# Norm sums on GpSimd, an identity made without it, and a Softmax issued step by step, in a cross-covariance attention and feed-forward kernel

## The chip, the cores and the metric

The kernel runs on one core of a Trainium2 chip. The metric is the device time of one execution in microseconds. The kernel before takes 575.51 us in the median of 9 runs (575.19 to 575.95).

## What is computed

Four batches of q, k and v come in, each 5824 x 256 in float32. Every column of q and k is normalized over the 5824 tokens, a 256 x 256 Softmax matrix is made from them, v is multiplied with it, and a feed-forward part with one product of two branches follows. In short:

```python
qn = q / (np.linalg.norm(q, axis=1, keepdims=True) + 1e-06)
kn = k / (np.linalg.norm(k, axis=1, keepdims=True) + 1e-06)
s = kn.transpose(0, 2, 1) @ qn / tau          # tau = 1
a = softmax(s, axis=-1)                       # with 1e-09 added to the sum
x = (v @ a).reshape(B * N, 256)
h = (x @ w1) * (x @ w2)                       # 256 -> 1024, twice
out = (h @ w3) @ w_out                        # 1024 -> 1024 -> 256
```

## The kernel before

Nothing non-linear stands between the weights, so they are folded. W = w3 @ w_out is made once (`w_unit`, L572). For each batch the Softmax matrix is multiplied into w1 and w2 (`fold`, L355), which gives Wf, 256 x 1024 twice. What is left for each token is the pair of products a and b of its row of v with the two halves of Wf, their product abs, and the output o = abs @ W.

The main loop (L636 to L647) runs over batches, over 12 chunks of tokens (11 of 512, a last one of 192) and over 8 column blocks j. One turn is a round. `emit_ab` (L419) issues two matmuls of 512 columns into a tile a and two into a tile b; ScalarE casts a to bfloat16 (L431), DVE multiplies it with b (L440). `emit_out` (L450) issues the four o matmuls of an earlier round (LAG = 2). After the last j of a chunk ScalarE and DVE each copy half of o out of PSUM (L486, L487), and the result is stored from SyncE's queue.

PSUM is shared out by tags: "ab" has four banks, which a, b, the folds and the small sums take in turn, "out" has three for o, and "G" has one for the score matrix.

Between the rounds the work for the next batch is put in. `make_agenda` (L587) writes a list of due times, with a cost for each item, and `run_due` (L381) issues what is due against a clock that is advanced by the reckoned TensorE time of what has been issued. The items are these.

- Loads of q, k and v pieces. They go over GpSimd's queue with a conversion to bfloat16. Ahead of each stands a one-element copy on GpSimd (`gate` L410, `hold` L415) that waits for a product of the current round or for a transposed piece of v, so a load doesn't start before its time. v is then transposed by DMA from SyncE's queue (L155 and following).
- Score units of the next batch (`score_units`, L167): two slots of tokens at a time, squares of q and k on ScalarE (L185), the products G = q^T k on TensorE (L188), and the squares added up on DVE in float32 (`acc`, L197). At batch index 0 they are due from 58.0 to 120.0 on the clock, later from 16.0 to 104.0 (t0, t1).
- Softmax units of the next batch (`soft_units`, L239), which the change touches.

The Softmax units of batches two to four are: `norms` (L263), one addition on DVE that leaves the squares of q and k of each of 128 partitions; `k_row` (L269), a float32 matmul with a matrix of ones that sums k's squares over partitions and spreads the sums over all of them, and four ScalarE steps (L274 to L277: logarithm, half of it exponentiated, again for the reciprocal) that turn it into kr; `q_sums` (L280), four float32 matmuls of one column for q's sums, followed by `q_norm` (L289: two ScalarE steps, two on DVE) that gives the scale r; `scaled`, two DVE multiplications of G with kr (`scale`, L302) and two ScalarE exponentials with scale r (L307); `sums` (L323, L329), the row sums over partitions and their reciprocal rs; and eight folds of two matmuls each (L344), copied out alternately by ScalarE (L351) and DVE (L353). They are due at t1 + 1.0, 3.5, 4.0, 8.0, 12.0, and the folds from t1 + 13.0 on, 0.9 apart.

The first batch has no earlier batch to hide behind. Its squares are made on TensorE (`squares`, L213) while q and k come in; the diagonals are picked out with an identity matrix. The identity is made on GpSimd (L502, a memset and a select) between the first four loads and the next ones. TensorE runs dummy matmuls (`busy`, L205) ahead of the first data, 14 of them.

Each engine works through its own instructions in the order of issue, so what stands behind a waiting instruction waits too.

Of the kernel before, what the change touches and what calls it, by code (L numbers as in the profile page):

```python
# [7 lines left out]


# [2 lines left out]
ALU = mybir.AluOpType  # L12
# [12 lines left out]
def kernel(  # L25
# [213 lines left out]
    def soft_units(n):  # L239
        st = {}  # L240

        def k_first():
            d = work.tile([P, CT, P], F32, tag="sq", name="dk", bufs=2)
            nc.vector.tensor_mul(d, S["k"], ident.unsqueeze(1).to_broadcast([P, CT, P]))
            st["ksq"] = d.rearrange("p c t -> p (c t)")

        def q_first():
            d = work.tile([P, CT, P], F32, tag="sq", name="dq", bufs=2)
            ss = work.tile([P, CT], F32, tag="ss0", name="ss0", bufs=1)
            for ct in range(CT):  # L250
                nc.vector.tensor_tensor_reduce(
                    out=d[:, ct, :], in0=S["q"][:, ct, :], in1=ident, scale=1.0, scalar=0.0,
                    op0=ALU.mult, op1=ALU.add, accum_out=ss[:, ct : ct + 1],
                )
            st["ss"] = ss

        def scaled_first():
            scale(0)
            q_norm(st["ss"])
            scale(1)  # L260
            exps()

        def norms():  # L263
            a1 = work.tile([P, 2, C], F32, tag="acc1", name=f"acc1_{n}", bufs=1)
            nc.vector.tensor_add(a1, accs[n][:, 0], accs[n][:, 1])
            st["ksq"] = a1[:, 1, :]
            st["qsq"] = a1[:, 0, :]

        def k_row():  # L269

            m = psum.tile([P, 512], F32, tag="ab", name=f"row_{n}", bufs=4)
            nc.tensor.matmul(m[:, :C], lhsT=ones_pp, rhs=st["ksq"], start=True, stop=True)  # L272
            kr = work.tile([P, C], F32, tag="kr", name=f"kr_{n}", bufs=1)
            nc.scalar.activation(out=kr, in_=m[:, :C], func=AF.Ln)  # L274
            nc.scalar.activation(out=kr, in_=kr, func=AF.Exp, scale=0.5)  # L275
            nc.scalar.activation(out=kr, in_=kr, func=AF.Ln, bias=eps_t)  # L276
            nc.scalar.activation(out=kr, in_=kr, func=AF.Exp, scale=-1.0)  # L277
            st["kr"] = kr

        def q_sums():  # L280
            m = psum.tile([P, 512], F32, tag="ab", name=f"ss_{n}", bufs=4)
            for ct in range(CT):
                nc.tensor.matmul(
                    m[:, ct : ct + 1], lhsT=st["qsq"][:, ct * P : (ct + 1) * P], rhs=ones_f,
                    start=(ct == 0), stop=(ct == CT - 1), skip_group_check=True,
                )
            q_norm(m[:, :CT])

        def q_norm(src):  # L289
            r = work.tile([P, CT], F32, tag="r", name=f"r_{n}", bufs=2)  # L290
            nc.scalar.activation(out=r, in_=src, func=AF.Ln)
            nc.scalar.activation(out=r, in_=r, func=AF.Exp, scale=0.5)
            nc.vector.tensor_scalar_add(r, r, 1e-6)
            nc.vector.reciprocal(r, r)
            if inv_tau != 1.0:
                nc.vector.tensor_scalar_mul(r, r, inv_tau)
            st["r"] = r

        def scale(ct):
            if ct == 0:  # L300
                st["s"] = work.tile([P, CT, C], F32, tag="s", name=f"s_{n}", bufs=1)
            nc.vector.tensor_mul(st["s"][:, ct, :], G_tiles[n][:, ct, :], st["kr"])  # L302

        def exps():
            e = work.tile([P, CT, C], BF16, tag="e", name=f"e_{n}", bufs=2)
            for ct in range(CT):
                nc.scalar.activation(  # L307
                    out=e[:, ct, :], in_=st["s"][:, ct, :], func=AF.Exp, scale=st["r"][:, ct : ct + 1]
                )
            st["e"] = e  # L310

        def scaled():
            for ct in range(CT):
                scale(ct)
            exps()

        def sum_mm(c2):
            if c2 == 0:
                st["sum"] = psum.tile([P, 512], F32, tag="out" if n == 0 else "ab", name=f"sum_{n}", bufs=3 if n == 0 else 4)
# [12 lines left out]

        def sums():
            sum_mm(0)
            sum_mm(1)

        def fold_mm(i, c2, tag="ab", on_act=None):
            h, rest = divmod(i, 4)
            w, c1 = divmod(rest, 2)
            if c2 == 0:  # L340
                st["fold", i] = psum.tile(
                    [P, 512], F32, tag=tag, name=f"fold_{n}_{i}", bufs={"ab": 4, "out": 3}[tag]
                )
            nc.tensor.matmul(  # L344
                st["fold", i], lhsT=st["e"][:, c2, c1 * P : (c1 + 1) * P], rhs=w12[:, c2, w, h * 512 : (h + 1) * 512],
                start=(c2 == 0), stop=(c2 == CT - 1),
            )
            if c2 == CT - 1:
                dst = Wf[n][:, c1, w, h * 512 : (h + 1) * 512]
                if on_act if on_act is not None else i % 2 == 0:  # L350
                    nc.scalar.activation(out=dst, in_=st["fold", i], func=AF.Copy, scale=st["rs"][:, c1 : c1 + 1])  # L351
                else:
                    nc.vector.tensor_scalar_mul(dst, st["fold", i], st["rs"][:, c1 : c1 + 1])  # L353

        def fold(i, tag="ab", on_act=None):  # L355
            fold_mm(i, 0, tag)
            fold_mm(i, 1, tag, i % 2 == 0 if on_act is None else on_act)

        def first_folds():
            sum_mm(0)  # L360
            fold_mm(0, 0)
            fold_mm(1, 0)
            sum_mm(1)
            fold_mm(0, 1)
            fold_mm(1, 1)
            fold(2)
            transpose_half_on_pe(0, 0, 0, False)
            fold(3, on_act=True)
            fold(4, "out", on_act=False)
            fold(5, "out")  # L370

        if n == 0:
            return [k_first, k_row, q_first, scaled_first, first_folds] + [lambda i=i: fold(i) for i in range(6, 8)]
        head = [(0.0, norms), (0.5, k_row), (0.4, q_sums)]
        return head + [(0.0, scaled), (0.2, sums)] + [(0.43, lambda i=i: fold(i)) for i in range(8)]


    clock = [0.0]
# [11 lines left out]
    def at(t, cost, fn):  # L390
        seq[0] += 1
        agenda.append((t, seq[0], cost, fn))
# [106 lines left out]
    busy(14)  # L499
    load_piece("k", 0, 0, (half,))  # L500
    load_piece("q", 0, 0, (half,))
    masks.make_identity(nc, ident)  # L502
    nc.vector.tensor_copy(ident_b, ident)
    w3_wout = vT_pool.tile([P, (NT - 1) * C], BF16, tag="vT", name="w3_wout")
    w3_bf = w3_wout[:, : FT * F].rearrange("p (j l) -> p j l", l=F)
    wout_sb = w3_wout[:, FT * F : FT * (F + D)].rearrange("p (l d) -> p l d", d=D)
# [2 lines left out]
    def transpose_w3():  # L509

        for h in range(FT // 2):
            m = in_pool.tile([P, 2, FT, P], BF16, tag="k", name=f"w3T_{h}", bufs=IN_BUFS["k"])
            nc.sync.dma_start_transpose(m, w3_bf[:, 2 * h : 2 * h + 2, :])
            w3T.append(m)

    w3r = moe_w3.rearrange("(jh jl) l -> jl jh l", jl=P)
    w1r = moe_w1.rearrange("(ch cl) f -> cl ch f", cl=P)
# [54 lines left out]
    def w_unit(jt):  # L572
# [10 lines left out]
        if jt == FT - 1:  # L583
            w_ready[0] = True


    def make_agenda(b):  # L587
        agenda.clear()
# [2 lines left out]
        if b == 0:  # L591
            for i in range(2):
                at(1.5 + 0.6 * i, 0.43, soft0[5 + i])
            at(4.0, 0.5, lambda: transpose_half_on_pe(0, 0, 1, False))
            at(7.0, 0.5, lambda: transpose_half_on_pe(0, 1, 0, True))
            at(8.0, 0.5, lambda: transpose_half_on_pe(0, 1, 1, False))
# [4 lines left out]
            moves = [("v", 0, 3, 29.0), ("qk", 1, 0, 38.0), ("qk", 1, 1, 43.0), ("v", 0, 4, 50.0), ("qk", 1, 2, 58.0)]  # L601
            moves += [("qk", 1, 3, 63.0), ("v", 0, 5, 70.0), ("qk", 1, 4, 81.0), ("qk", 1, 5, 87.0)]
            moves += [("v", 1, 0, 96.0), ("v", 1, 1, 106.0), ("v", 1, 2, 116.0), ("qk", 2, 0, 126.0)]
            t0, t1 = 58.0, 120.0
        else:
            moves = [("v", b, 3, 1.0), ("qk", n, 1, 10.0), ("qk", n, 2, 17.0), ("v", b, 4, 26.0), ("qk", n, 3, 38.0)]
            moves += [("v", b, 5, 46.0), ("qk", n, 4, 58.0), ("qk", n, 5, 66.0)]
# [20 lines left out]
        for i, (cst, fn) in enumerate(units):  # L628
            at(t0 + (t1 - t0) * i / len(units), cst, fn)
        soft = soft_units(n)  # L630
        ts = [t1 + 1.0, t1 + 3.5, t1 + 4.0, t1 + 8.0, t1 + 12.0] + [t1 + 13.0 + 0.9 * i for i in range(8)]
        for t, (cst, fn) in zip(ts, soft):
            at(t, cst, fn)
        agenda.sort()

    for b in range(B):  # L636
# [48 lines left out]
```

## Time and profile before

| | |
|---|---|
| median of 9 runs | 575.51 us |
| profiled execution, its own time | 575.19 us |
| its span, first to last instruction | 573.4 us |
| granted TensorE clock | 0.999 |
| DVE busy / ScalarE busy / GpSimd busy | 65% / 59% / 13% |
| the cast of a (L431), one of 128 x 512 | 0.58 us |
| the product abs (L440), one of 128 x 512 | 0.69 us |
| k steps L274, L275, L276, L277 | 0.38, 0.42, 0.51, 0.42 us |
| an exponential L307 | 0.50 us |
| a multiplication of G with kr, L302 | 0.42 us |
| a fold copied out, ScalarE / DVE | 0.69 / 0.75 us |
| norms' addition L265 | 0.68 us |

The span counts from the first to the last instruction of the program; the execution's own time has 1.8 us more around it. A row of the order of time gives the start, the length, the engine, the line, the operation, the tiles written and read, and how many instructions of the kind follow one another; in brackets is the engine's idle time before it and what ended it. PE is TensorE, PEld its weight loads, ACT is ScalarE, POOL is GpSimd. The end of a matmul is modelled, so a gap of TensorE is read from the distance between the starts of matmuls, not from its busy time. In the chain of waits TensorE has 91% of the span, DMA 5%, which is the head, and every other engine 1% or less.

### The profile page before, as it was taken

What the parts mean: (1) busy time and instruction counts of PE and PEld (TensorE: products, weight loads), DVE (VectorE), ACT (ScalarE), POOL (GpSimd) and SP (SyncE); (2) the same over time, 40 slices, a digit from 0 to 9 for tenths busy, and PEclk for the clock granted to TensorE, in tenths of its full rate; (3) what the DMA queues carried; (4) which work ended last, traced back from release to release, by engine and by line L of the source; (5) the groups of instructions that cost most, each with busy time, mean ns of one, the idle gap of its engine ahead of it and who ended that gap; (6) DMA issues with size and microseconds to landing.
All of it is one profiled execution on the core that took longest, in us unless ns stands there. A gap on an engine that the chain in (4) does not pass through costs nothing.

```text
span 573.4 us, 10131 instructions
## 1 busy us (share of the span) xinstructions
PE 562.0 (98%) x3766; PEld 356.8 (62%) x3766; DVE 374.5 (65%) x597; ACT 337.9 (59%) x624; POOL 72.3 (13%) x162
## 2 busy tenths in 40 slices
PE   8889999999999999999999999999999999999997
PEld 4755566776666666666666666666665666665665
DVE  0047644787967567887776567778876656565564
ACT  0046534777766567776765567767765554454453
POOL 5240020202120111121000012021100000000000
PEclk9999999999999999999999999999999999999999
DMA  8999959779575696495661595665740325221011
GB/s 163 211 194 209 190 98 234 179 168 217 136 177 114 123 209 149 92 186 126 145 147 52 115 208 127 137 139 120 182 110 38 85 73 146 64 63 74 38 70 59
DMA packets 74560, 76.93 MB, mean 134 GB/s; under 512 B 54160, under 2 KB 58256, under 8 KB 74512
## 3 DMA queue, kind: packets, MB, share of 16 engines
q0 software_dynamic: 15504, 39.46, 39.0%
q1 hardware_dynamic: 58784, 36.64, 21.3%
q8 instruction: 29, 0.48, 0.3%
q10 hardware_dynamic: 224, 0.20, 0.1%
q14 instruction: 19, 0.16, 0.1%
HBM read 78.91 MB, written 23.86 MB: 179 GB/s over the span
## 4 chain that ended last, share of the span: by engine, by line
PE 91%; DMA 5%; ACT 1%; issue 1%; DVE 1%; POOL 1%; ACTq 0%; POOLq 0%
PE o L466 27%; PE a L425 27%; PE b L425 27%; PE G L188 5%; DMA k<-in_k_dram 5%; PE fold L344 2%; PE w L575 1%; ACT as L431 1%; PE row L272 0%; POOL k L109 0%; DVE abs L440 0%; DVE osb L487 0%; POOL q L109 0%; ACT kr L276 0%; ACT kr L275 0%
## 5 line engine op out<-in xcount | busy, mean ns | idle before, releaser
L440 DVE TENSOR_TENSOR abs<-as,b 128x512 bf16<-128x512 bf16 x336 | 229.9, 686 | 140.3 <-ACT as L431 128.6
L431 ACT CAST as<-a 128x512 bf16<-128x512 f32 (+1 forms) x384 | 215.3, 562 | 177.7 <-PE a L425 86.7
L425 PEld LDWEIGHTS <-Wf 128*128 128x128 bf16 x1536 | 149.1, 98 | 102.5 <-issue 2.6
L466 PE MATMUL o<-W_sb,abs 128*128 128x256 bf16 x1376 | 209.7, 273 | 0.5 <-ACT osb L486 0.4
L425 PE MATMUL a<-vT,Wf 128*128 128x512 bf16 x704 | 209.4, 379 | 0.3
L425 PE MATMUL b<-vT,Wf 128*128 128x512 bf16 x704 | 209.4, 379 | 0.0
L466 PEld LDWEIGHTS <-abs 128*128 128x128 bf16 x1376 | 134.5, 98 | 82.0 <-issue 0.6
L197 DVE TENSOR_TENSOR acc<-acc,sq 128x1024 f32<-128x1024 f32 x66 | 80.4, 1219 | 0.8 <-ACT sq L185 0.8
L188 PE MATMUL G<-k,q 128*128 128x256 bf16 x276 | 49.6, 273 | 0.0
L185 ACT ACTIVATE sq<-q 128x512 f32<-128x512 bf16 x66 | 41.8, 633 | 0.0
L185 ACT ACTIVATE sq<-k 128x512 f32<-128x512 bf16 x66 | 41.6, 630 | 0.0
L413 POOL COPY gate_t<-abs 1x1 bf16<-1x1 bf16 x39 | 13.0, 332 | 183.1 <-DVE abs L440 182.5
L487 DVE COPY osb<-o 128x512 f32<-128x512 f32 x44 | 30.1, 684 | 0.0
L188 PEld LDWEIGHTS <-q 128*128 128x128 bf16 x276 | 27.0, 98 | 3.1
L486 ACT COPY osb<-o 128x512 f32<-128x512 f32 x44 | 25.7, 585 | 4.6 <-PE o L466 2.6
L417 POOL COPY gate_t<-vT 1x1 bf16<-1x1 bf16 x17 | 4.7, 274 | 179.7 <-DMA vT<-v 144.3
L274 ACT ACTIVATE kr<-row 128x256 f32<-128x256 f32 x4 | 1.5, 384 | 33.6 <-PE row L272 33.6
L109 POOL DMA_DIRECT2D q<-in_q_dram x29 | 15.6, 539 | 12.6 <-DMA k<-in_k_dram 5.5
L344 PE MATMUL fold<-w,e 128*128 128x512 bf16 x64 | 17.0, 378 | 0.0
L351 ACT ACTIVATE Wf<-fold,rs 128x512 bf16<-128x512 f32 x16 | 10.9, 686 | 7.2 <-PE fold L344 4.9
L109 POOL DMA_DIRECT2D k<-in_k_dram x25 | 13.8, 550 | 4.8 <-DMA k<-in_k_dram 2.0
L109 POOL DMA_DIRECT2D v<-in_v_dram x25 | 13.5, 542 | 3.8 <-issue 2.5
(87 smaller groups left out, 218.9 us busy)
## 6 DMA issues: line engine op xcount, KB each, us to landing
out_dram<-osb SPq DMA_DIRECT2D x44, 512.0 KB, 3.0
k<-in_k_dram POOLq DMA_DIRECT2D x19, 512.0 KB, 8.5
v<-in_v_dram POOLq DMA_DIRECT2D x19, 512.0 KB, 5.1
q<-in_q_dram POOLq DMA_DIRECT2D x18, 512.0 KB, 6.4
w_wout<-in_moe_w_dram POOLq DMA_DIRECT2D x1, 2048.0 KB, 23.3
k<-in_k_dram POOLq DMA_DIRECT2D x4, 320.0 KB, 9.4
v<-in_v_dram POOLq DMA_DIRECT2D x4, 320.0 KB, 5.3
q<-in_q_dram POOLq DMA_DIRECT2D x4, 256.0 KB, 11.9
```

Of the source, the lines that this page charges most:

```text
L109: nc.gpsimd.dma_start(out=pieces[nm, n, pi][:, lo:hi, :], in_=qk_main[nm, n][0][:, pi * PIECE + lo : pi * PIECE + hi, :])
L185: nc.scalar.activation(out=dst[:, :, part, :], in_=src[:, o : o + 2, :], func=AF.Square)
L188: nc.tensor.matmul(G[:, ct, :], lhsT=qt[:, i, ct * P : (ct + 1) * P], rhs=kt[:, i, :], start=(pr == 0 and part == 0 and ct == 0), stop=(pr ...
L197: nc.vector.tensor_add(accs[n], accs[n], sqs[0])
L344: nc.tensor.matmul(st["fold", i], lhsT=st["e"][:, c2, c1 * P : (c1 + 1) * P], rhs=w12[:, c2, w, h * 512 : (h + 1) * 512], start=(c2 == 0), ...
L413: nc.gpsimd.tensor_copy(gate_t, last_ab[0][:1, :1])
L425: nc.tensor.matmul(t[:, :n], lhsT=Wf[b][:, ct, w, j * P : (j + 1) * P], rhs=rhs_of(b, c, ct), start=(ct == 0), stop=(ct == CT - 1),)
L431: nc.scalar.copy(a_sb[:, :n], tiles[0][:, :n])
L440: nc.vector.tensor_mul(ab, a_sb, tiles[1])
L466: nc.tensor.matmul(tl[h][:, o, :], lhsT=lhsT, rhs=W_sb[:, j, :], start=(j == 0 and o == 0), stop=(j == FT - 1 and (small or o == 1)), skip ...
L486: nc.scalar.copy(o[:, 0:2, :], tl[0])
L487: nc.vector.tensor_copy(o[:, 2:4, :], tl[1])
```

## The change

1. For batches two to four `norms` sends its result to GpSimd, which sums it over the partitions and writes the sums to all partitions (`partition_all_reduce`, 128 x 512 in float32). The row matmul and the four one-column matmuls are gone there. k's four steps read that sum; q's sums come from its diagonal on DVE (two masked reductions with the identity), as in the first batch. The tile of the sum takes the buffer of s.
2. [...]A sum of one column (`load_library`) is put into the agenda of the first batch at time 0; in GpSimd's order it stands behind the load of w3 and ahead of the first gate.
3. The identity is made from a running sum along the row of ones on DVE, a matmul of one partition that turns the row into a column, and a comparison on DVE. On TensorE that matmul stands behind the 14 dummy matmuls. GpSimd's two instructions between the loads are gone.
4. The Softmax of batches two to four is one instruction at a time: each k step, each scale and each exponential is an item of the agenda, 1.3 apart. The first k step is due 6 units after norms, 8 in batch two. The row sums of the exponentials use G's bank in place of one of "ab".
5. Times: at batch index 0 the scores are due from 57.0 to 115.5. The folds start at t1 + 17.5 (t1 + 19.5 in batch two), 0.85 apart, which is later than before by 4.2 to 4.5 units for batches three and four and by 1.7 to 2.0 for batch two.

```diff
         def norms():
             a1 = work.tile([P, 2, C], F32, tag="acc1", name=f"acc1_{n}", bufs=1)
             nc.vector.tensor_add(a1, accs[n][:, 0], accs[n][:, 1])
-            st["ksq"] = a1[:, 1, :]
-            st["qsq"] = a1[:, 0, :]
+            tot = work.tile([P, 2, C], F32, tag="s", name=f"tot_{n}", bufs=1)
+            nc.gpsimd.partition_all_reduce(
+                tot.rearrange("p w c -> p (w c)"), a1.rearrange("p w c -> p (w c)"), P, ReduceOp.add
+            )
+            st["tot"] = tot
...
+        def k_step(i):
+            kr = st["kr"]
+            nc.scalar.activation(
+                out=kr, in_=kr if i else st["row"], func=(AF.Ln, AF.Exp)[i % 2],
+                scale=(1.0, 0.5, 1.0, -1.0)[i], bias=eps_t if i == 2 else 0.0,
+            )
...
         def q_sums():
-            m = psum.tile([P, 512], F32, tag="ab", name=f"ss_{n}", bufs=4)
-            for ct in range(CT):
-                nc.tensor.matmul(
-                    m[:, ct : ct + 1], lhsT=st["qsq"][:, ct * P : (ct + 1) * P], rhs=ones_f,
-                    start=(ct == 0), stop=(ct == CT - 1), skip_group_check=True,
-                )
-            q_norm(m[:, :CT])
+            st["ss"] = diagonal(st["tot"][:, 0, :].rearrange("p (c t) -> p c t", t=P))
...
-        head = [(0.0, norms), (0.5, k_row), (0.4, q_sums)]
-        return head + [(0.0, scaled), (0.2, sums)] + [(0.43, lambda i=i: fold(i)) for i in range(8)]
+        return (
+            [(0.0, 0.0, norms), (0.0, 6.0, k_row)]
+            + [(0.0, 6.0 + 1.3 * i, lambda i=i: k_step(i)) for i in range(4)]
+            + [(0.0, 6.5, q_sums), (0.0, 9.3, lambda: q_norm(st["ss"]))]
+            + [(0.0, 11.3 + 1.3 * ct, lambda ct=ct: scale(ct)) for ct in range(CT)]
+            + [(0.0, 12.0 + 1.3 * ct, lambda ct=ct: exps(ct)) for ct in range(CT)]
+            + [(0.2, 15.5, sums)]
+            + [(0.43, 16.5 + 0.85 * i, lambda i=i: fold(i)) for i in range(8)]
+        )
...
-    masks.make_identity(nc, ident)
-    nc.vector.tensor_copy(ident_b, ident)
...
+    idx = work.tile([P, P], F32, tag="sq", name="idx", bufs=2)
+    nc.vector.tensor_tensor_scan(idx, ones_pp, ones_pp, 0.0, ALU.mult, ALU.add)
+    turned = psum.tile([P, 512], F32, tag="ab", name="turned", bufs=4)
+    nc.tensor.matmul(turned[:, :1], lhsT=idx[:1, :], rhs=ones_f[:1, :], start=True, stop=True)
+    number = work.tile([P, 1], F32, tag="number", name="number", bufs=1)
+    nc.vector.tensor_copy(number, turned[:, :1])
+    nc.vector.tensor_scalar(out=ident, in0=idx, scalar1=number, scalar2=None, op0=ALU.is_equal)
+    nc.vector.tensor_copy(ident_b, ident)
...
+    def load_library():
+
+        m = work.tile([P, 1], F32, tag="lib", name="lib", bufs=1)
+        nc.gpsimd.partition_all_reduce(m, ones_f, P, ReduceOp.add)
...
+            at(0.0, 0.0, load_library)
...
-            t0, t1 = 58.0, 120.0
+            t0, t1 = 57.0, 115.5
...
-        ts = [t1 + 1.0, t1 + 3.5, t1 + 4.0, t1 + 8.0, t1 + 12.0] + [t1 + 13.0 + 0.9 * i for i in range(8)]
-        for t, (cst, fn) in zip(ts, soft):
-            at(t, cst, fn)
+        for i, (cst, t, fn) in enumerate(soft):
+            at(t1 + 1.0 + t + (2.0 if b == 0 and i > 0 else 0.0), cst, fn)
```

More of the change, by code (lines that the diff above doesn't have):

```diff
@@ L5 @@
 from concourse import bass_utils, mybir
-from concourse import masks
+from concourse.bass_isa import ReduceOp
 from concourse._compat import with_exitstack
@@ L245, in k_first @@
             st["ksq"] = d.rearrange("p c t -> p (c t)")
-        def q_first():
-            d = work.tile([P, CT, P], F32, tag="sq", name="dq", bufs=2)
-            ss = work.tile([P, CT], F32, tag="ss0", name="ss0", bufs=1)
-            for ct in range(CT):
-                nc.vector.tensor_tensor_reduce(
-                    out=d[:, ct, :], in0=S["q"][:, ct, :], in1=ident, scale=1.0, scalar=0.0,
-                    op0=ALU.mult, op1=ALU.add, accum_out=ss[:, ct : ct + 1],
-                )
-            st["ss"] = ss
         def scaled_first():
@@ L260, in scaled_first @@
             scale(1)
-            exps()
+            exps(0)
+            exps(1)
         def norms():
@@ L265, in norms @@
             nc.vector.tensor_add(a1, accs[n][:, 0], accs[n][:, 1])
-            st["ksq"] = a1[:, 1, :]
-            st["qsq"] = a1[:, 0, :]
-        def k_row():
[L271 to L278, printed above, removed]
@@ L280, in q_sums @@
-        def q_sums():
-            m = psum.tile([P, 512], F32, tag="ab", name=f"ss_{n}", bufs=4)
-            for ct in range(CT):
-                nc.tensor.matmul(
-                    m[:, ct : ct + 1], lhsT=st["qsq"][:, ct * P : (ct + 1) * P], rhs=ones_f,
-                    start=(ct == 0), stop=(ct == CT - 1), skip_group_check=True,
-                )
-            q_norm(m[:, :CT])
+            tot = work.tile([P, 2, C], F32, tag="s", name=f"tot_{n}", bufs=1)
+            nc.gpsimd.partition_all_reduce(
+                tot.rearrange("p w c -> p (w c)"), a1.rearrange("p w c -> p (w c)"), P, ReduceOp.add
+            )
@@ new lines, in norms @@
+            st["tot"] = tot
+        def k_row():
+            if n == 0:
+                m = psum.tile([P, 512], F32, tag="ab", name=f"row_{n}", bufs=4)
+                nc.tensor.matmul(m[:, :C], lhsT=ones_pp, rhs=st["ksq"], start=True, stop=True)
+                src = m[:, :C]
+            else:
+                src = st["tot"][:, 1, :]
+            st["row"] = src
+            st["kr"] = work.tile([P, C], F32, tag="kr", name=f"kr_{n}", bufs=1)
+            if n == 0:
+                for i in range(4):
+                    k_step(i)
@@ new lines, in k_step, with diagonal @@
+        def k_step(i):
[4 more added lines that the diff above has]
+            )
+        def diagonal(src):
+            d = work.tile([P, CT, P], F32, tag="sq", name=f"dq_{n}", bufs=2)
+            ss = work.tile([P, CT], F32, tag="ss0", name=f"ss0_{n}", bufs=1)
+            for ct in range(CT):
+                nc.vector.tensor_tensor_reduce(
+                    out=d[:, ct, :], in0=src[:, ct, :], in1=ident, scale=1.0, scalar=0.0,
+                    op0=ALU.mult, op1=ALU.add, accum_out=ss[:, ct : ct + 1],
+                )
+            return ss
@@ L289, in q_norm, with q_first @@
+        def q_first():
+            st["ss"] = diagonal(S["q"])
+        def q_sums():
+            st["ss"] = diagonal(st["tot"][:, 0, :].rearrange("p (c t) -> p c t", t=P))
         def q_norm(src):
@@ L302, in scale, with exps @@
             nc.vector.tensor_mul(st["s"][:, ct, :], G_tiles[n][:, ct, :], st["kr"])
[L304 to L315, printed above, removed]
+        def exps(ct):
+            if ct == 0:
+                st["e"] = work.tile([P, CT, C], BF16, tag="e", name=f"e_{n}", bufs=2)
+            nc.scalar.activation(
+                out=st["e"][:, ct, :], in_=st["s"][:, ct, :], func=AF.Exp, scale=st["r"][:, ct : ct + 1]
+            )
         def sum_mm(c2):
             if c2 == 0:
-                st["sum"] = psum.tile([P, 512], F32, tag="out" if n == 0 else "ab", name=f"sum_{n}", bufs=3 if n == 0 else 4)
+                st["sum"] = psum.tile([P, 512], F32, tag="out" if n == 0 else "G", name=f"sum_{n}", bufs=3 if n == 0 else 1)
                 Wf[n] = wf_pool.tile([P, CT, 2, F], BF16, tag="Wf", name=f"Wf_{n}")
@@ L373, in soft_units @@
             return [k_first, k_row, q_first, scaled_first, first_folds] + [lambda i=i: fold(i) for i in range(6, 8)]
-        head = [(0.0, norms), (0.5, k_row), (0.4, q_sums)]
-        return head + [(0.0, scaled), (0.2, sums)] + [(0.43, lambda i=i: fold(i)) for i in range(8)]
+        return (
[6 more added lines that the diff above has]
+            + [(0.43, 16.5 + 0.85 * i, lambda i=i: fold(i)) for i in range(8)]
+        )
     clock = [0.0]
```

## The prediction

> **What bounds the kernel now.** I read the page's busy times and slices first, then the stretches of the head, then the order of time around the three later Softmax stages, and GpSimd's own timeline.
>
> ```profile
> span 573.4 us, 10131 instructions
> PE 562.0 (98%) x3766; PEld 356.8 (62%) x3766; DVE 374.5 (65%) x597; ACT 337.9 (59%) x624; POOL 72.3 (13%) x162
> PE   8889999999999999999999999999999999999997
> ```
>
> TensorE has something in flight 98% of the time at a granted clock of 1.00, so the time is TensorE's work and the few places where it waits. Three slices of 8 are the head. In it the DMA engines are the limit, as two stretches (busy of PE, PEld, DVE, ACT, POOL, then clock, DMA share, GB/s) show:
>
> ```profile
> 4.00:6.00 2.00, 2.00 (x6) 0.68 (x5) 0.39 (x2) 0.00 (x0) 2.00 (x5) 1.00 1.11 205
> 10.00:12.00 2.00, 1.42 (x17) 1.07 (x15) 0.17 (x1) 0.00 (x0) 0.53 (x1) 1.00 1.08 215
> ```
>
> The DMA share is full from 4 us on. Next, TensorE and ScalarE at batch two's Softmax (order of time; start, length, engine, line):
>
> ```profile
> 163.32 0.60 PE L466 MATMUL o<-W_sb,abs 128*128 128x256 bf16 x4
> ...
> 163.76 0.60 PE L272 MATMUL row<-acc,ones_pp 128*128 128x256 f32 x2
> ...
> 164.19 0.50 PE L283 MATMUL ss<-ones_f,acc 128*128 128x1 f32 x4
> ...
> 164.56 0.59 PE L425 MATMUL a<-vT,Wf 128*128 128x512 bf16 x2
> ...
> 167.52 0.38 PE L466 MATMUL o<-W_sb,abs 128*128 128x256 bf16 x2 [0.39 <-ACT osb L486]
> ```
>
> A normal round (a, b, o) takes 1.30 us, and after o the next a follows in 0.44. Here a starts at 164.56 and not at 163.76: row and ss cost 0.80 us. In batches three and four the same pairs of lines give 0.80 as well (291.03 to 291.83, 424.94 to 425.74). The o at 167.52 has its first half at 166.75 and waited for osb, which stood behind six ScalarE steps: matmul starts there are 0.55 apart beyond their length.
>
> **What the Trainium skill says.** "GPSIMD Engine Reference", section 2.1: the first call to a freshly loaded library pays about 6 us that no instruction shows. No instruction of the trace before shows it. Same page, section 3.1: a one-input pass over 512 elements takes 769 ns; section 3.2: a partition-axis tensor_reduce of 128x2048 takes 247.7 us. The trace has no GpSimd reduction at all. "SBUF — State Buffer", section "SBUF: two separate sides": a DVE instruction with two SBUF inputs and a GpSimd one that reads SBUF exclude each other. The trace agrees:
>
> ```profile
> 160.47 1.22 DVE L197 TENSOR_TENSOR acc<-acc,sq 128x1024 f32<-128x1024 f32 x1
> 160.66 1.07 POOL L413 COPY gate_t<-abs 1x1 bf16<-1x1 bf16 x1
> 161.67 0.53 POOL L109 DMA_DIRECT2D v<-in_v_dram  x1
> ```
>
> The 1x1 copy takes 0.18 elsewhere; here it ends with the acc addition.
>
> **The change, part by part.**
>
> *Removed from TensorE.* Row and ss, three batches: 3 x 0.80 = 2.40 us, on the path.
>
> *The block of six ScalarE steps* (164.39 to 166.50) is spread over rounds. A round gives ScalarE 1.30 us, its cast takes 0.58, a step 0.38 to 0.51: they fit. The 0.55 at batch two's osb goes. In batches three and four that block cost TensorE nothing measurable, so nothing is gained there.
>
> *The all-reduce, 128x512, on GpSimd.* Unknown. From below: one pass, 0.77 us. From above: the quoted tensor_reduce by columns, 247.7/4 = 62 us. [...]I take an estimate of five passes, 3.8 us. What covers it is the gap between the norms' addition and the first k step, which waits for it on ScalarE with the casts queued behind. By the rows of before (casts 1.30 apart, no row matmul): batch four, addition ends 424.18, the cast ahead of the step ends 427.46: 3.3 us; batch three 290.26 to 294.84: 4.6. Batch two: GpSimd stands behind the v load, whose gate waits for a transpose and which issues at 161.67, so it is free at 162.2 (161.3 if no acc addition holds the copy), and the step is due behind osb at 165.6: 3.4 to 4.3. TensorE further bears a late cast: in batches three and four the cast behind the exponentials starts 1.17 late (297.58, due 296.41) with no gap in the matmuls. So the sum is free up to about 4.5 (batch four), 4.6 and 5.8 us, and 3.8 costs 0. It can't gain by itself. Behind it in GpSimd's queue stand gates and loads of the next batch (q at 171.18 and 292.33), needed 16 us or more into the next batch: 0. DVE has no addition with two SBUF inputs left in that window: 0.
>
> *The diagonals on DVE* (q sums): two masked reductions of 0.29 with two reads of 0.09, some 0.6 us in a DVE that is 65% busy there. A late product is borne like a late cast: 0.
>
> *The exponentials, one at a time.* In the order of the engines, batches three and four now have on ScalarE cast, e, cast, e, cast and on DVE product, s, product, s, product, each e waiting for the s that stands behind the product of the cast just ahead. The rows of before show the price of one such turn:
>
> ```profile
> 296.31 0.75 DVE L302 TENSOR_TENSOR s<-G,kr 128x256 f32<-128x256 f32 x2
> ...
> 296.77 0.91 ACT L307 ACTIVATE e<-s,r 128x256 bf16<-128x256 f32 x2 [1.09 <-DVE s L302]
> ...
> 297.58 1.05 ACT L431 CAST as<-a 128x512 bf16<-128x512 f32 x2
> ```
>
> ScalarE idles 1.09 in the turn. Before, there is one turn per batch; after, two: 2 x (0.58 + 1.09 + 0.50) = 4.34 us in two rounds of 2.60, so the third cast comes 1.74 late, and up to 0.35 more where osb and a k step precede. TensorE bears 1.17. Left: 0.6 in batch four, 0.9 in batch three, of which overlapping ends (casts start 0.1 before e ends) give back 0.1 to 0.2 each: -1.2 us together. In batch two s stands one product earlier, no turn: 0.
>
> *Folds, 2 to 4.5 us later in the agenda, and sum in G's bank.* Batches three and four lose 0.47 us in the first group of three folds, ScalarE waiting 1.09 for rs, which stood behind osb on DVE. In batch three no osb lies there after: +0.3; in batch four rs still stands behind a late product: 0. Folds now run into the last, short chunk, whose rounds leave DVE little room (0.50 of 0.55), and in batch two the last three stand right before the next batch: between +0.6 (batch two lost 0.9 in that stretch) and -0.6; I take 0. Scores of batch two end 4.5 us of agenda earlier; their fourth q piece is then due near 139.1, landed 134.8; its k 140.1 against 138.3: 0.
>
> *Head.* The identity leaves GpSimd's queue: six loads issue 0.57 us sooner (3.46, not 4.03). They only queue behind transfers that already fill the engines: 0; +0.57 if that cover were gone. The scan on DVE (0.17 to 0.3 by the memset and the masked reduction) is done by 2 us; the small matmul sits on TensorE behind the 14 warm ones and costs 0.1 to 0.2 ahead of sqk, which the 0.58 wait for q at 8.60 hides. Its copy on DVE holds the memset of k's edge from 4.40 to some 7.4; that DMA issues at 14.96. The identity is first read at 32.22.
>
> *The library* is loaded behind the last issue (35.98) where GpSimd next works at 72.35: 35 us cover 6 us and a one-column sum. Its fetch may delay w3 (landed 59.24), whose first transposed piece lands at 63.22, 3.0 before its matmul: 0.
>
> Sum: 2.40 + 0.55 + 0.30 - 1.20 = 2.05 us. The profiled execution took 575.19 (span 573.4 and 1.8 around it), so 573.1 for it; the runs' median is 575.51, 0.32 above, so **573.5**.
>
> **The rivals.**
>
> *A: the turns cost nothing* (TensorE bears more than the 1.17 seen): 2.40 + 0.55 + 0.30 = 3.25, less 0 to 1, and with the short chunk's 0.6: 572.0. For it: 1.17 is only what was tried. Against: four PSUM buffers are two rounds.
>
> *B: the gain is handed back* by deeper stalls in turns and folds, DVE being as full as TensorE in the short chunk: another 1.5 to 2: 575.2.
>
> *C, slower: the all-reduce outlasts its cover.* ScalarE stands at the first k step, casts behind it, TensorE stops when four buffers are full. Beyond 4.5 us each microsecond costs nearly one per batch; at 5.6 the gain is gone, beyond 6.1 it is slower; at 8 us (3.4 + 2.2 + 3.5) = 9.1: 582.6. For it: the only partition reduction with a price is far dearer. Against: 512 columns are few passes.
>
> *That it doesn't do what it says*: the engines' order shows the matmuls gone and the sum on GpSimd, so no.
>
> **How the numbers follow.** Likeliest 0.46 (572.6 to 574.3), A 0.18, B 0.20, C 0.16. Two runs of this kernel can be told apart by about 0.2%, 1.15 us: faster is below 574.36. Faster 0.64, same 0.20, slower 0.16. The range, 571.3 to 576.0, takes in A and B and the beginning of C.
>
> **What would show it.** Row and ss gone and o to a at 0.44; the wait of the first k step for the all-reduce near 0 (C: microseconds, casts behind it); the e rows with two idle times near 1.1 in batches three and four, and gaps of TensorE two rounds later (A: none); first loads as late to land as before. A sum over 6 us makes the prediction wrong.

## The result, and the profile after

The changed kernel takes 572.96 us in the median of 9 runs (572.90 to 573.24), against 575.51 us before (29 runs). The ratio is 0.9955, 95% interval 0.9947 to 0.9964, so it is faster by 2.1 to 3.1 us. Two more executions of it are on record, of 572.76 and 575.73 us; the median of all eleven is the same. Forecast were 573.5 us and a gain of 2.05 us for the profiled execution; its own time is 573.03 us against 575.19, a gain of 2.16. By the medians the gain is 2.55.

The page's head and TensorE's slices, which answer to those of before:

```profile
span 571.3 us, 10102 instructions
PE 560.3 (98%) x3750; PEld 354.8 (62%) x3750; DVE 377.2 (66%) x612; ACT 337.3 (59%) x624; POOL 83.4 (15%) x164
PE   8889999999999999999999999999999999999997
```

TensorE is as full as before and has 1.7 us less work. GpSimd has 11.1 us more and DVE 2.7 us more. In the two stretches of the head (PE, PEld, DVE, ACT, POOL, clock, DMA share, GB/s) the DMA engines carry about what they carried before, 202 and 211 GB/s for 205 and 215.

```profile
4.00:6.00 2.00, 2.00 (x6) 0.69 (x5) 0.00 (x0) 0.00 (x0) 1.91 (x5) 1.00 1.10 202
10.00:12.00 2.00, 2.00 (x26) 1.85 (x24) 0.00 (x0) 0.00 (x0) 0.09 (x2) 1.00 1.05 211
```

TensorE at batch two's Softmax in order of time: after an o the next a follows in 0.44 us (162.27 to 162.71), and the round with osb in it (166.17, 166.61) has no gap either.

```profile
162.27 0.60 PE L479 MATMUL o<-W_sb,abs 128*128 128x256 bf16 x4
162.71 0.59 PE L438 MATMUL a<-vT,Wf 128*128 128x512 bf16 x2
...
166.17 0.60 PE L479 MATMUL o<-W_sb,abs 128*128 128x256 bf16 x4
166.61 0.59 PE L438 MATMUL a<-vT,Wf 128*128 128x512 bf16 x2
```

Where the time went shows best when the same round is found in both traces (start of its first matmul, us):

| round | before | after | difference | what lies between |
|---|---|---|---|---|
| first of batch one | 39.97 | 40.35 | +0.37 | head |
| first of batch two | 182.84 | 181.78 | -1.07 | W; batch two's scores and Softmax |
| second of batch two's last chunk | 312.24 | 310.21 | -2.03 | batch three's Softmax |
| fifth of batch three's tenth chunk | 425.74 | 422.94 | -2.81 | batch four's norms |
| first of batch four | 449.90 | 447.73 | -2.17 | the rest of batch four's Softmax and folds |
| end of the span | 573.43 | 571.26 | -2.16 | |

Batch four is the odd one: 0.78 us is won at its norms and 0.64 us given back before the batch begins.

### The profile page after: what moved, and what is told of

Its sections match the earlier page's. It is cut to its first block, busy times and chain, and to the rows that moved or that the text cites. A ratio compares the mean times of both kernels' runs of the same rounds, so it can differ in the third digit from the quotient of the medians.

```text
span 571.3 us, 10102 instructions
## 1 busy us (share of the span) xinstructions
PE 560.3 (98%) x3750; PEld 354.8 (62%) x3750; DVE 377.2 (66%) x612; ACT 337.3 (59%) x624; POOL 83.4 (15%) x164
## 4 chain that ended last, share of the span: by engine, by line
PE 91%; DMA 5%; ACT 1%; DVE 1%; issue 1%; POOL 1%; ACTq 0%; POOLq 0%
PE o L479 27%; PE a L438 27%; PE b L438 27%; PE G L188 5%; DMA k<-in_k_dram 5%; PE fold L349 2%; PE w L596 1%; ACT as L444 1%; DVE abs L453 0%; ACT kr L279 0%; POOL k L109 0%; POOL q L109 0%; ACT e L318 0%; DVE s L313 0%; PE sqk L221 0%
```

## The experiments

Each time below is a median of its runs, the kernel before ran beside it on the same chip, and the edits are to the changed kernel unless it says otherwise.

**The identity on GpSimd again.** The identity is made with the memset and select between the first loads; the sum stays on GpSimd.

```diff
+    masks.make_identity(nc, ident)
+    nc.vector.tensor_copy(ident_b, ident)
...
-    nc.vector.tensor_tensor_scan(idx, ones_pp, ones_pp, 0.0, ALU.mult, ALU.add)
...
```

> The changed kernel with the identity made on GpSimd again, between the loads. Theory (the head is bound by the DMA engines): 573.0 us, within 0.2 of the changed kernel. Rival 1 (the earlier issue was a gain of up to 0.57): 573.5. Rival 2 (the new identity made the head longer, as the 0.37 later first round of the changed kernel's trace could mean): 572.7.

Measured: 581.57 us (581.09 to 582.16), ratio 1.0104 (1.0091 to 1.0117), 8.6 us slower than the changed kernel. Every expectation missed. GpSimd's order of time in this kernel:

```profile
3.47 0.24 POOL masks.py:197 MEMSET ident<- 128x128 f32 x1
12.97 0.28 POOL masks.py:199 TENSOR_SCALAR_AFFINE_SELECT ident<-ident 128x128 f32<-128x128 f32 x1 [9.26 <-issue]
13.23 0.74 POOL L110 DMA_DIRECT2D k<-in_k_dram  x1
...
52.64 0.40 POOL L605 PARTITION_ALL_REDUCE lib<-ones_f  x1 [8.48 <-DVE Wf L359]
```

The select waits 9.26 us for nothing that the profile shows, and the next load of k issues at 13.23, not at 3.47; the first round starts 7.39 us later, which is most of the 8.06 us between the two profiled executions. The one-column sum waits 8.48 us once more, at a time when GpSimd has nothing else to do. In the kernel before the same select started 0.08 us after its memset ended, and in the changed kernel the one-column sum starts 0.13 us after the issue ahead of it:

```profile
36.20 0.95 POOL L572 DMA_DIRECT2D w_wout<-in_moe_w_dram  x1
37.28 0.40 POOL L610 PARTITION_ALL_REDUCE lib<-ones_f  x1
```

So neither operation waits in a program that has only one of them, and both do in the program that has both. A possible reading is that each needs a library of its own, and that a program's only one is in place already; the runs show the waits, not the mechanism. With this the third part of the change is not a matter of 0.57 us in the head: without it, with the identity made by the select, the first part would make the kernel 6 us slower than before.

**Without the early one-column sum.**

```diff
-            at(0.0, 0.0, load_library)
```

> The changed kernel without the early one-column sum[...]; nothing else differs. Theory (from the profiles: where a program uses one library only, its first use waits 0.1 us, and 9.26 and 8.48 us only where it uses two): the early call does nothing, 573.0 us within 0.4, and the first sum of 128x512 starts right behind the v load and takes about 3.2 us. Rival (a library is fetched at its first use, as the Trainium skill's 6 us or the 9 us of the two-library program): the first sum of batch two ends 6 to 9 us later, where its cover is already used up, so 578.6 to 582.

Measured: 573.02 us (572.80 to 573.90), ratio 0.9952 (0.9938 to 0.9966). The theory holds. GpSimd in this kernel, where the first 128 x 512 sum is also the program's first sum:

```profile
161.24 0.53 POOL L109 DMA_DIRECT2D v<-in_v_dram  x1 [0.31 <-issue]
161.97 3.18 POOL L258 PARTITION_ALL_REDUCE tot<-acc  x1 [0.20 <-issue]
```

Its first use waits 0.20 us. The early call does nothing here, and no run shows that anything is loaded for this sum.

**The identity alone.** The kernel before with only the new identity.

```diff
-    masks.make_identity(nc, ident)
...
+    nc.vector.tensor_tensor_scan(idx, ones_pp, ones_pp, 0.0, ALU.mult, ALU.add)
...
```

> The kernel before with only the identity changed (scan, turned number, comparison, on DVE, after the first loads are issued), Softmax as it was. Theory (prediction's head: the loads issue 0.57 us sooner behind transfers that are the limit): 575.5 us within 0.3, the fifth piece of k landing within 0.3 of 31.29. Rival (the sooner loads are worth their 0.57): 574.9. Second rival (the head's 0.37 later first round in the changed kernel is this part's doing): 575.9.

Measured: 575.65 us (575.30 to 576.06), ratio 1.0003 (0.9995 to 1.0011): no gain larger than 0.3 us and no loss larger than 0.6. The sooner loads gain nothing that can be seen, as forecast; the second rival's loss of 0.4 is not excluded. In its profiled execution, one of its longer ones, the fifth piece's first matmul starts at 32.03 and not within 0.3 of 31.34, and the first round is 0.92 later; over the profiles of this study that have the new identity and the loads at 3.5, the first round starts between 40.01 and 40.90, where the one profile of the kernel before has 39.97. Whether the head has become some tenths longer stays open.

**The norms on TensorE again.** Row and ss are matmuls as before, every Softmax step stays an item of its own, and no sum is on GpSimd.

```diff
-            nc.gpsimd.partition_all_reduce(
-                tot.rearrange("p w c -> p (w c)"), a1.rearrange("p w c -> p (w c)"), P, ReduceOp.add
-            )
...
+            nc.tensor.matmul(m[:, :C], lhsT=ones_pp, rhs=st["ksq"], start=True, stop=True)
...
```

> The changed kernel with the row and column sums on TensorE again, all else kept (steps one at a time, folds later, new identity; no library). Theory (the removed matmuls are the gain): 0.80 us more per batch, 575.4. Rival (issuing the Softmax step by step is the gain): 573.0 to 573.5.

Measured: 574.78 us (574.38 to 577.28, 21 runs), ratio 0.9990 (0.9984 to 0.9997), 1.8 us above the changed kernel. The lower of the two expectations is out, the higher one is 0.6 too high. Its trace has the 0.80 between o and a back in each batch (165.16 to 165.95 for batch two), and 0.05, 0.34 and 0.39 of it come back later in the three batches, where the folds fall otherwise. So the matmuls are 1.8 us of the gain of 2.5, net of what comes back; the other 0.7 to 0.8 us is left in this kernel and belongs to the other parts.

**The steps in blocks again.** The sum stays on GpSimd, but the four k steps with q's steps, and the two multiplications with the two exponentials, are due together.

```diff
-            + [(0.0, 6.0 + 1.3 * i, lambda i=i: k_step(i)) for i in range(4)]
...
+            + [(0.0, 6.0, lambda i=i: k_step(i)) for i in range(4)]
+            + [(0.0, 6.0, q_sums), (0.0, 6.0, lambda: q_norm(st["ss"]))]
...
+            + [(0.0, 11.3, lambda ct=ct: exps(ct)) for ct in range(CT)]
```

> The changed kernel with the k steps, the q steps and the scales with exponentials issued in blocks again, at the first due time of each. Theory: batch two pays for the block at its output copy, up to 0.55, batches three and four save the second turn between ScalarE and DVE, 0.33 and 0.19 by the changed kernel's matmul gaps: 573.0, within 0.4. Rival (step by step carries the gain): 574.5 or more.

Measured: 573.81 us, with runs from 572.98 to 574.86; ratio 0.9969 (0.9957 to 0.9981). The median lies between the two expectations and fits neither; the two shortest of the five runs are at the theory's 573.0. The profiled execution, the longest of the five, has a wait that the changed kernel's profile has not, TensorE and batch two's scores:

```profile
138.75 0.38 PE L479 MATMUL o<-W_sb,abs 128*128 128x256 bf16 x2
140.80 0.60 PE L188 MATMUL G<-k,q 128*128 128x256 bf16 x4 [1.67 <-DMA k<-in_k_dram]
```

A piece of k lands late and costs 1.8 us. Leaving that out, its rounds against the changed kernel's give +0.87 us in batch two (0.63 at osb), -0.3 in batch three and -0.7 in batch four: nearly zero together, as the theory has it. By this profile, spreading the steps gains in batch two what it loses in three and four.

**The sum made twice.**

```diff
+            nc.gpsimd.partition_all_reduce(
+                tot.rearrange("p w c -> p (w c)"), a1.rearrange("p w c -> p (w c)"), P, ReduceOp.add
+            )
```

> The changed kernel with the sum over partitions made twice, one after the other, so that it takes 6.4 us for 3.2. Theory (cover of about 3.3, 4.6 and 3.3 us for batches two, three and four, and 1.4 us that TensorE bears): 1.7 + 0.4 + 1.7 = 3.8 us more, 576.8, the first k step waiting on ScalarE. Rival (the cover is longer than reckoned): 573.0 to 574.

Measured: 579.81 us (578.49 to 582.39), ratio 1.0073 (1.0054 to 1.0092). The profiled execution has the same late piece of k (1.7 us). Without it the three stages are 2.14, 0.92 and 1.95 us longer, 5.0 together where 3.8 were expected: right in kind, 0.3 to 0.5 short in each batch. ScalarE at batch two, in this kernel:

```profile
167.17 0.58 ACT L502 COPY osb<-o 128x512 f32<-128x512 f32 x1
170.70 0.42 ACT L282 ACTIVATE kr<-tot 128x256 f32<-128x256 f32 x1 [2.95 <-POOL tot L261]
171.02 0.57 ACT L447 CAST as<-a 128x512 bf16<-128x512 f32 x1
```

This is the prediction's slower rival brought about: the k step stands 2.95 us with the casts behind it. The cast starts at 171.02 where it was due at 167.82 (1.30 after the one ahead at 166.52), 3.20 late; TensorE loses 1.85 in that round and 0.29 in the next. So it bears about 1.35 us of a late cast before it stops.

**The k and q load gated a round earlier.** The fourth transfer of k and q for batch two is moved from 81 to 78 in the agenda.

```diff
-            moves += [("qk", 1, 3, 63.0), ("v", 0, 5, 70.0), ("qk", 1, 4, 81.0), ("qk", 1, 5, 87.0)]
+            moves += [("qk", 1, 3, 63.0), ("v", 0, 5, 70.0), ("qk", 1, 4, 78.0), ("qk", 1, 5, 87.0)]
```

> The changed kernel with batch two's fourth pair of q and k pieces gated on a product one round earlier (moved at 78 instead of 81 of the agenda). Theory: the spread between executions of the changed kernel and its relatives (573.0, with some at 574.4 to 575.7) is that piece of k, which lands 1.3 to 2 us ahead of its use at best; issued one round or more earlier it is never late, so all runs lie at 573.0 within 0.4 and none at 574.4 or above; in the profile k lands 1 to 2 us earlier and no square of k waits for its transfer. Rival (the spread has another cause): runs at 574.4 and above stay, about one in four.

Measured: 573.30 us (572.95 to 574.51), ratio 0.9957 (0.9944 to 0.9970). The theory was not tested, because the edit did not move the load. GpSimd in this kernel:

```profile
127.14 0.18 POOL L430 COPY gate_t<-vTt 1x1 bf16<-1x1 bf16 x1 [13.86 <-DVE acc L197]
...
128.38 0.54 POOL L109 DMA_DIRECT2D k<-in_k_dram  x1
```

GpSimd stood 13.86 us at the gate ahead of it, the one for v's last transposed piece, so k issues at 128.38 where it issued at 128.18. One of the five runs is above 574.4, as in the rival.

**Asking for that piece later.** Instead the score units that use it are due up to 1.5 later (batch two only).

```diff
-            at(t0 + (t1 - t0) * i / len(units), cst, fn)
+            w = 48 if b == 0 else len(units)
+            late = 1.5 * (len(units) - i) / (len(units) - w) if i >= w else 0.0
+            at(t0 + (t1 - t0) * i / len(units) + late, cst, fn)
```

> The changed kernel with batch two's scores of its fifth and sixth pieces (units 48 to 68) due 1.5 later at first and 0 later at the end, so that the piece of k that was late by 1.9 us in some profiles is asked for about one round later; all else as it is. Theory (that piece makes the spread): 573.0 within 0.3 in every run, none at 574.0 or above. Rival (the spread is something else, or the denser scores cost): some runs at 574 or above, or a median above 573.4.

Measured: 573.12 us, all runs from 572.72 to 573.27; ratio 0.9958 (0.9945 to 0.9972). The square of that piece starts at 140.21, 1.0 later than in the changed kernel, and nothing is lost. The median doesn't move; the longer runs are absent here, which fits the late piece as their cause but, with five runs, doesn't prove it.

The traces show how the piece comes to be late. Its load stands on GpSimd behind a one-element copy, the gate. In eight of the eleven profiles of the changed kernel and its variants that copy takes 0.18 us, and k lands in time. In the other three (the steps in blocks, the sum twice, the identity on GpSimd) the copy starts just after a large addition on DVE, takes 1.15 to 1.23 us, and k issues about 1 us later and lands too late. In the kernel with the steps in blocks:

```profile
127.58 1.22 DVE L197 TENSOR_TENSOR acc<-acc,sq 128x1024 f32<-128x1024 f32 x1
127.67 1.17 POOL L426 COPY gate_t<-abs 1x1 bf16<-1x1 bf16 x1
```

In the changed kernel the copy starts at 127.17, ahead of that addition at 127.46. A few tenths of a microsecond decide which comes first. So a run of any of these kernels can be longer by 1.7 or 1.8 us for this alone; that all the longer runs are such runs is not shown.

**The exponentials one round later, batches three and four.**

```diff
+        late = 1.3 if n > 1 else 0.0
...
-            + [(0.0, 12.0 + 1.3 * ct, lambda ct=ct: exps(ct)) for ct in range(CT)]
+            + [(0.0, 12.0 + late + 1.3 * ct, lambda ct=ct: exps(ct)) for ct in range(CT)]
...
```

The sum and the folds are shifted by the same 1.3.

> The changed kernel with the exponentials, the sum and the folds of batches three and four due 1.3 later, so that in the order of the engines each exponential stands one product behind its s, and not just behind the s that waits for that product. Theory (a turn costs TensorE what the trace showed after it, 0.33 in batch three and 0.19 in batch four): the waits of 1.09 us for s are gone and 0.5 us of matmul gaps with them, less up to 0.3 for folds that go deeper into the short chunk: 572.5 to 573.0. Rival (the turns cost the 1.2 us of the prediction): 571.8.

Measured: 572.50 us (572.09 to 573.74), ratio 0.9943 (0.9930 to 0.9956); beside it on the chip the kernel without the early sum took 573.02. The theory's range holds and the rival's 571.8 does not. ScalarE at batch three's exponentials in the changed kernel:

```profile
298.54 0.58 ACT L444 CAST as<-a 128x512 bf16<-128x512 f32 x1
300.21 0.51 ACT L318 ACTIVATE e<-s,r 128x256 bf16<-128x256 f32 x1 [1.09 <-DVE s L313]
300.62 0.57 ACT L444 CAST as<-a 128x512 bf16<-128x512 f32 x1
302.28 0.51 ACT L318 ACTIVATE e<-s,r 128x256 bf16<-128x256 f32 x1 [1.09 <-DVE s L313]
302.69 1.05 ACT L444 CAST as<-a 128x512 bf16<-128x512 f32 x2
```

The same place and engine in the kernel of this experiment:

```profile
299.60 0.58 ACT L445 CAST as<-a 128x512 bf16<-128x512 f32 x1 [0.57 <-PE a L439]
300.12 0.51 ACT L318 ACTIVATE e<-s,r 128x256 bf16<-128x256 f32 x1
300.90 0.58 ACT L445 CAST as<-a 128x512 bf16<-128x512 f32 x1 [0.28 <-PE a L439]
301.38 0.51 ACT L318 ACTIVATE e<-s,r 128x256 bf16<-128x256 f32 x1
```

With s one product ahead, the two waits of 1.09 are gone and every cast comes in its round. Not all of the gain comes from that, because the edit moves the folds as well. A gap of TensorE is counted here as the distance between two starts beyond what the same matmul takes in an undisturbed round. The eleventh chunks lose 0.29 us (batch three) and 0.64 (batch four) in gaps in the changed kernel and nothing in this one, but about 0.48 of the 0.64 lay in the first group of folds, behind rs; and the last chunks lose 0.22 and 0.06 more than in the changed kernel.

**The scores of batches three and four sooner.** They end at 101.4 of the agenda instead of 104.0, and Softmax and folds with them.

```diff
-            t0, t1 = 16.0, 104.0
+            t0, t1 = 16.0, 101.4
```

> The changed kernel with the score units of batches three and four ending at 101.4 of the agenda instead of 104.0, so that their Softmax and folds come two rounds earlier and batch four's last folds lie ahead of the short chunk. Theory (the folds in the short chunk are where batch four gave back some 0.5 us): 572.5, batch four's last chunk without its gaps of 0.44 and 0.18. Rival (the short chunk costs the same with fewer folds in it, or the denser scores cost as much): 573.0 or above.

Measured: 573.77 us (573.69 to 574.49), ratio 0.9967 (0.9954 to 0.9979). The rival's number holds, though not its first reason: the gaps of batch four's short chunk do shrink, from 0.84 us to 0.36. But the folds and the row sum in the chunk ahead now lose 1.40 where they lost 0.64, and in batch three 0.75 where they lost 0.29. The gaps move with the folds; they don't go. Whether the denser scores add to it stays open.

**Together.** The later exponentials, the piece of k asked for later, and no early sum.

```diff
+        late = 1.3 if n > 1 else 0.0
...
+            w = 48 if b == 0 else len(units)
...
-            at(0.0, 0.0, load_library)
```

> The changed kernel with three edits of the runs before: exponentials, sum and folds of batches three and four 1.3 later, the early one-column sum left out, the fourth piece's scores of batch two 1.5 later. Theory: the gain of the first edit alone remains, 572.3 to 572.6, and no run over 573.3. Rival: the edits hinder each other, 573.0 or above.

Measured: 572.58 us (572.28 to 572.77), ratio 0.9949 (0.9937 to 0.9962), 0.54 below the kernel of the experiment on that piece, which ran beside it and differs in the exponentials and the idle early sum. Medians of 572.5 and 572.6 are the lowest of the study; against the changed kernel's 572.96 that is less than 0.1%.

## Why the prediction was right, step by step

**Row and ss, 2.40 us: right.** The 0.80 is gone in each batch, and putting the matmuls back brings it back.

**Batch two's block at osb, 0.55: right.** The round with osb in it is 0.58 us shorter than before, and the kernel with the steps in blocks loses 0.63 there. But by its profile that kernel gains as much in batches three and four, so issuing step by step gained nothing as a whole that the runs show.

**The all-reduce, 3.8 us and free: right, with less to spare than stated.** It takes 3.19 to 3.23 us, three times (GpSimd in the changed kernel, batch two):

```profile
161.98 0.53 POOL L109 DMA_DIRECT2D v<-in_v_dram  x1 [0.31 <-issue]
162.54 3.19 POOL L258 PARTITION_ALL_REDUCE tot<-acc  x1
```

It ends at 165.73 and the first k step starts at 165.77, right behind osb: batch two's cover was used to the last tenth. In batch four it is the same (425.50 and 425.54); in batch three 1.15 us are left. The forecast's five passes were a guess, and that it came within 0.6 us is luck; its covers, 3.4 to 4.3, 4.6 and 3.3 us, measure 3.2, 4.4 and 3.3 here and were the part that decided. The prices set beside the guess, from the Trainium skill's "GPSIMD Engine Reference", were no guide: the 769 ns of section 3.1 are that page's best case, a tight loop over 512 elements, and the 247.7 us of section 3.2, as an estimate 62 us for 512 columns, would have made the kernel far slower. A partition all-reduce isn't priced by either. The slower rival was a true danger, as the doubled sum shows: this sum lay at the edge of its cover, with what TensorE bears of a late cast as the only reserve.

**The turns of the exponentials, 1.2 us: the mechanism right, the size wrong.** Both batches have the two waits of 1.09, at the places named. The third cast comes 1.69 us late in batch three (302.69; the casts ahead are 1.30 apart from 295.80 on, which puts it at 301.00) and 1.56 in batch four, where the forecast had 1.74 to 2.09. TensorE then loses 0.33 and 0.19 in matmul starts, so it bears 1.36 and 1.37, not 1.17: that had only been the largest lateness seen without a gap, and was used as a limit. The doubled sum gives 1.35 at another place. The experiment that undid the turns gained 0.5 us by the medians. This is near the 0.52 of the gaps, but in part by chance: as said above, some of it came from the fold group behind rs, and the short chunks took some back. By the gaps the term is 0.5, not 1.2.

**rs in batch three, 0.30: right in kind.** The stall of 0.47 before its fold group is gone whole. In batch four it stays, as forecast: TensorE loses 0.48 us in the fold group, and ScalarE waits 1.20 us for rs.

**The short chunk, 0 in a range of 0.6 either way: a loss of 0.5 us in batch four.** There the folds reach into the short chunk and osb falls among its casts. The same round on TensorE in the kernel before and in the changed one:

```profile
447.80 0.33 PE L425 MATMUL a<-vTt,Wf 128*128 128x192 bf16 x2
...
448.37 0.33 PE L425 MATMUL a<-vTt,Wf 128*128 128x192 bf16 x2
```

```profile
445.18 0.33 PE L438 MATMUL a<-vTt,Wf 128*128 128x192 bf16 x2
445.44 0.33 PE L438 MATMUL b<-vTt,Wf 128*128 128x192 bf16 x2
445.69 0.28 PE L479 MATMUL o<-W_sb,abs 128*128 128x256 bf16 x1
446.24 0.33 PE L438 MATMUL a<-vTt,Wf 128*128 128x192 bf16 x2 [0.27 <-ACT as L444]
```

The round took 0.57 us and takes 1.06. Over the chunk the gaps grow from 0.36 us to 0.84, which with the turns' 0.19 is the 0.64 that batch four gives back; in batches two and three the last chunk loses less than 0.1 more than before. Two errors of about half a microsecond cancel: turns too dear by 0.7, the short chunk too cheap by 0.5.

**The head, 0: right within the noise, two of its steps not.** The identity alone measures 0.1 us, within its interval of nothing. The running sum takes DVE 0.42 us, not 0.17 to 0.3. And the first sqk starts at 7.45 where it started at 6.60, the first sqq at 9.21 for 8.61: more than the 0.1 to 0.2 that the small matmul was to cost, and more than the wait of 0.58 us at 8.60 could hide. By 28 us the two kernels are level (sqk at 28.02 and 28.05).

**The library, 0: right, for a wrong reason.** 35 us of cover were named for the 6 us that the Trainium skill's "GPSIMD Engine Reference", section 2.1, gives for a freshly loaded library. No such wait exists in this program, early call or none. It exists in a program that uses both kinds of GpSimd operation, at 9.26 and 8.48 us; there the measurements are above the page's figure. What kept the term at 0 is that the select had gone, which the prediction did not name as a condition.

**The pieces of k, 0: right in the median, too sure.** The margin named for the fourth k piece was 140.1 less 138.3. In the changed kernel the piece lands at 138.64 and its square starts at 139.20, so 0.56 us are left. In two profiles of relatives of the kernel, with the same score times, that is used up and 1.7 and 1.8 us are lost. The prediction had read the cause, a gate's copy that stands behind an addition on DVE, at batch two's v load, and did not apply it here.

By these sizes the sum is 2.40 + 0.55 + 0.47 - 0.52 - 0.5, less 0.25 to 0.37 in the head: 2.0 to 2.15 us, against 2.16 in the spans. The mechanisms were read rightly, but that the total of 2.05 came so close is luck: the turns, the short chunk and the head were off by 0.7, 0.5 and 0.3 us, and these errors cancel.

## What to carry to other kernels

A reduction over partitions can leave a full TensorE for an idle GpSimd if the work between its input and its first reader is longer than it is: read that cover at the place where it is shortest. Here a sum longer by 3.2 us cost 2.14, 0.92 and 1.95 us in the three batches. When one engine's item needs the result of another's, put one routine item of the second engine between them in program order; two items each waiting just behind the other's routine work make both engines idle in turn. And a gap at the end of a stage moves with the work that causes it, so starting that work sooner need not remove it.

## What the runs showed of the hardware

The partition all-reduce on GpSimd takes 3.19 to 3.23 us for 128 x 512 in float32 and 0.40 us for 128 x 1. A running sum along the row takes DVE 0.42 us for 128 x 128. A select on GpSimd and a partition all-reduce in one program waited 9.26 and 8.48 us before their first use; each alone in a program waited 0.1 to 0.2 us. A one-element copy on GpSimd took 0.18 us, and 1.15 to 1.23 where it started just after a two-input addition of 1.22 us on DVE. With four banks for a and b, TensorE bore a cast 1.35 to 1.37 us late, a little over one round of 1.30, before a matmul started later (1.69 late and 0.33 lost, 1.56 and 0.19, 3.20 and 1.85).
